# Joins of the weights' conversion moved behind masking and low parts in a linear-attention and two-MoE kernel

## The chip, the cores and the metric

The kernel runs on one core of a Trainium2 chip. The metric is the time in microseconds that the device takes for one execution; the median of three runs is compared. Names of engines in the rows: PE is TensorE's matmul and PEld its weight load, DVE is VectorE, ACT is ScalarE, POOL is GpSimd, SP is SyncE, which issues most of the transfers.

## What is computed

Three stages follow each other. A linear attention with decay (2 batches, 8 heads, 768 steps, head dimension 48) gives 1536 rows of 384. A feed-forward layer with a leaky activation (384 to 2048 to 384) follows, and then a routed layer with 8 experts (384 to 1024 to 384), each token going to its best expert. Only the first two stages are touched by the change:

```python
for t in range(S):
    kt, vt, rt = (k[:, :, t], v[:, :, t], r[:, :, t])
    cur = np.einsum('bhd,bhe->bhde', u[None] * kt, vt)
    y[:, :, t] = np.einsum('bhd,bhde->bhe', rt, state + cur)
    state = w[None, :, :, None] * state + np.einsum('bhd,bhe->bhde', kt, vt)
...
h = x @ w_in
g = np.maximum(h, 0.0) + alpha * np.minimum(h, 0.0)
return (g @ w_out).astype(np.float32)
```

## The kernel before

The 1536 tokens are cut into 12 tiles of 128 and three blocks of four tiles. Attention of the first four tiles runs ahead; then the feed-forward layer goes over block 0, 1 and 2, each in 16 slices of 128 hidden units (so 48 slices), and the attention of the next block's tiles is threaded into the slices of the block before it. In each slice `moe1_slice` has TensorE make nine products into a PSUM bank h (three passes over high and low parts, L608), ScalarE scales and clips them into ng (L624), VectorE multiplies and adds (L627), ScalarE casts the high part gh (L628), VectorE subtracts to get the low part gl (L631). The slice then runs the second product (L593, twelve matmuls) of the slice two before. There are two banks h, so the first products of slice g wait for gl of slice g - 2.

Every product takes float32 numbers as a high and a low part. For the weights these parts are made on the chip, once, by `convert_moe1`: 256 hidden units make one q (0 to 7), part 0 is the first layer's weight, part 1 the second layer's. A conversion has six steps:

- step 0 (L359): ScalarE scales the high words into the scratch tile rowss
- step 1: nothing
- step 2 (L362): VectorE shifts and masks in rowss
- step 3 (L365), the first join: VectorE brings in bits of the low words, still in rowss
- step 4 (L368), the second join: VectorE puts the number together in the raw weight tile rm
- step 5: ScalarE casts the high part into wm (L371) and GpSimd subtracts to get the low part there (L372)

From q = 4 on all conversions use the same half of rowss, so step 0 of one waits for step 4 of the one before.

The order in each queue is that in which the code is written out; nothing reorders it. A slice has five places for other work: its start, behind ng, behind gh, behind gl, and behind the second product. The table CONVERT gives, for the conversion whose base slice is `at` (2q for part 1, 2q - 3 for part 0), six numbers, one for each step: number p means slice at + p // 5, and p % 5 is the place in the order just named. A conversion without an entry takes OTHERS. At one place the conversion's steps come first and the attention's behind them. The attention of a tile has phases in fixed slices: the score is made and masked (L213 and L216, `score0`, behind gh) in slices 2, 5, 8 and 11; the finished tile is transposed (px, L265, end of slices 5, 8, 13 and 14) and put into xh and xl (L273, L274, start of the next). The score's two banks, px, pr (L186), pk (L198), py (L222, L229) and pg (L240) share two banks of PSUM in turn.

Of the kernel before, what the change touches and what calls it, by code (L numbers as in the profile page):

```python
# [23 lines left out]
def kernel(  # L24
# [918 lines left out]
    with tc.manual_schedule():  # L943
# [137 lines left out]
        c1[5]()  # L1081


        CONVERT = {0: (0, 0, 0, 0, 2, 3), 1: (-5, 1, 1, 1, 5, 9), 2: (-4, -2, -1, 2, 3, 7), 4: (-1, 0, 2, 5, 6, 7), 5: (-4, -1, 0, 1, 4, 6), 3: (-4, 0, 2, 5, 5, 7), 6: (-3, -1, 2, 4, 5, 7), 7: (-6, -6, -4, -2, 2, 4)}
        OTHERS = (-1, -1, 0, 0, 0, 5)
        work = [([], [], [], [], [], []) for _ in range(NBLK * NFT)]
        for q in range(NW):
            for x in range(2):
# [5 lines left out]
                def step(n, c=c, q=q, x=x):  # L1094
                    if n == 0:
                        c.extend(convert_moe1(q, x, nc.gpsimd))
                    c[n]()
                for n, p in enumerate(CONVERT.get(at, OTHERS)):
                    g = at + p // 5
# [144 lines left out]
```

## Time and profile before

| what | us |
|---|---|
| median of three runs | 464.07 |
| lowest and highest run | 461.83, 465.22 |
| the profiled execution | 462.03 |
| its span on the core | 459.9 |
| TensorE busy in the span | 424.0 (92%) |
| VectorE busy in the span | 267.9 (58%) |
| ScalarE busy in the span | 201.7 (44%) |
| GpSimd busy in the span | 160.0 (35%) |

Durations in the profile come from the one profiled execution, whose time stands beside its span; the 2.1 us between them lie around the span. The shares are means over stages with different limits, so a stage is read from windows of its own.

### The profile page before, as it was taken

The page shows a single profiled execution, that of the slowest core. Times are in us where ns is not written, and L with a number is a line of the kernel's source. Part 1 is how long each engine was busy: PE and PEld are TensorE (multiplying, and loading weights), DVE is VectorE, ACT ScalarE, POOL GpSimd, SP SyncE. Part 2 cuts the span into 40 slices and gives each one's busy share as a digit, 9 for nine tenths or more (in the row PEclk, how much of TensorE's full clock was granted, in tenths as well). Part 3 has the DMA queues.
Part 4 walks back from the last instruction along what each step waited for, and adds up shares of the span by engine and source line. Part 5 has one row for each costly group of instructions (what it writes and reads, how often), then busy time and mean ns, then how long its engine had stood idle before and what let it go on. Part 6 is the DMA issues. An engine that isn't in the chain of part 4 may idle for free. (4 is left out here: it accounts for less than half of the span.)

```text
span 459.9 us, 7878 instructions
## 1 busy us (share of the span) xinstructions
PE 424.0 (92%) x3012; PEld 363.5 (79%) x3012; DVE 267.9 (58%) x475; ACT 201.7 (44%) x335; POOL 160.0 (35%) x141
## 2 busy tenths in 40 slices
PE   8877989699899999999999999999998887899985
PEld 7765778488788988988898889987966465798774
DVE  6888998999753444345433575354535355443651
ACT  1236545354444333323254444334636366543861
POOL 7845467454440231100300040031407145521660
PEclk9998999989999999999999999999999899899999
DMA  7989950649610105200900020016748728901900
GB/s 130 231 250 280 337 149 3 169 145 358 205 36 17 38 16 201 92 0 6 340 1 1 0 75 12 1 45 192 285 148 281 261 62 298 323 34 41 323 16 19
DMA packets 70513, 62.36 MB, mean 136 GB/s; under 512 B 41837, under 2 KB 58131, under 8 KB 70464
## 3 DMA queue, kind: packets, MB, share of 16 engines
q1 hardware_dynamic: 68832, 57.29, 40.4%
q0 software_dynamic: 1632, 4.40, 2.5%
q8 instruction: 32, 0.52, 0.5%
q14 instruction: 17, 0.14, 0.1%
HBM read 49.99 MB, written 12.18 MB: 135 GB/s over the span
## 5 line engine op out<-in xcount | busy, mean ns | idle before, releaser
L593 PE MATMUL acc<-wm,gh 128*128 128x384 f32 x384 | 100.8, 343 | 0.5 <-POOL wm L372 0.5
L608 PE MATMUL h<-xh,wm 128*128 128x512 f32 (+1 forms) x294 | 87.4, 407 | 3.6 <-DVE gl L631 3.6
L627 DVE SCALAR_TENSOR_TENSOR h<-ng,sign,h 128x512 f32<-128x512 f32 x48 | 36.1, 752 | 67.9 <-ACT ng L624 67.9
L593 PEld LDWEIGHTS acc<-wm,gh 128*128 128x128 f32 x384 | 68.8, 188 | 4.9 <-POOL wm L372 1.1
L593 PE MATMUL acc<-wm,gl 128*128 128x384 f32 x192 | 64.8, 338 | 0.0
L608 PEld LDWEIGHTS h<-xh,wm 128*128 128x128 f32 x294 | 53.2, 192 | 13.3 <-issue 2.9
L788 PE MATMUL eh<-we,d 128*128 128x512 f32 x198 | 54.5, 420 | 5.4 <-ACT we L687 3.1
L690 POOL TENSOR_TENSOR we<-re,we 128x768 fp32r<-128x768 f32 x21 | 41.7, 1984 | 50.8 <-ACT we L687 36.0
L624 ACT ACTIVATE ng<-h,slope 128x512 f32<-128x512 f32 x48 | 33.1, 690 | 57.3 <-PE h L608 57.3
L628 ACT CAST gh<-h 128x512 fp32r<-128x512 f32 x48 | 28.1, 586 | 63.3 <-DVE h L627 63.3
L687 ACT CAST we<-re 128x768 fp32r<-128x768 f32 x64 | 50.6, 839 | 1.8 <-ACTq L934 1.4
L690 DVE TENSOR_TENSOR we<-re,we 128x768 fp32r<-128x768 f32 x43 | 40.7, 973 | 17.8 <-ACT we L687 16.8
L788 PEld LDWEIGHTS eh<-we,d 128*128 128x128 f32 x198 | 37.2, 197 | 17.3 <-issue 9.9
L372 POOL TENSOR_TENSOR wm<-rm,wm 128x768 fp32r<-128x768 f32 x16 | 32.2, 2012 | 46.8 <-ACT wm L371 42.9
L526 POOL DMA_INDIRECT disp<-rows,sl x12 | 12.6, 1048 | 100.0 <-DVE run L552 64.4
L608 PE MATMUL h<-xl,wm 128*128 128x512 f32 (+1 forms) x147 | 42.9, 401 | 0.0
L631 DVE TENSOR_TENSOR gl<-h,gh 128x512 fp32r<-128x512 f32 x48 | 33.0, 687 | 15.6 <-ACT gh L628 15.0
L805 DVE TENSOR_TENSOR gl<-pht,gh 128x512 fp32r<-128x512 f32 x22 | 15.2, 692 | 44.1 <-ACT gh L804 42.4
L813 PE MATMUL ey<-we,gh 128*128 128x384 f32 x176 | 37.7, 346 | 0.0
L593 PEld LDWEIGHTS acc<-wm,gl 128*128 128x128 f32 x192 | 36.1, 188 | 0.0
L608 PEld LDWEIGHTS h<-xl,wm 128*128 128x128 f32 x147 | 28.2, 194 | 6.9 <-DVE xl L274 0.2
L813 PEld LDWEIGHTS ey<-we,gh 128*128 128x128 f32 x176 | 29.7, 189 | 0.4 <-ACT gh L804 0.4
(200 smaller groups left out, 612.8 us busy)
## 6 DMA issues: line engine op xcount, KB each, us to landing
re<-in_moe_w_dram SPq DMA_DIRECT2D x32, 768.0 KB, 6.6
rm<-in_moe_w_in_dram SPq DMA_DIRECT2D x8, 768.0 KB, 5.9
rm<-in_moe_w_out_dram SPq DMA_DIRECT2D x8, 768.0 KB, 6.7
disp<-rowss SPq DMA_DIRECT2D x1, 4825.0 KB
drow<-disp SPq DMA_DIRECT2D x7, 579.0 KB, 8.2
out_dram<-rowss SPq DMA_DIRECT2D x1, 2304.0 KB, 22.7
kn<-in_k_dram SPq DMA_DIRECT2D x10, 192.0 KB, 7.6
rn<-in_r_dram SPq DMA_DIRECT2D x10, 192.0 KB, 3.6
```

What stands on the lines that cost most here:

```text
L372: eng.tensor_tensor(lo, low.bitcast(F32), hi.bitcast(F32), ALU.subtract)
L593: nc.tensor.matmul(accs[(blk, s)], gs[g][a][:, s * P:(s + 1) * P], wout[b][:, ft % 2, :], start=(ft == 0 and n == 0), stop=(ft == NFT - 1 ...
L608: nc.tensor.matmul(phs[g][:, cols[0]:cols[1]], win[a][:, c, o:o + P], xs[b][:, c, cols[0]:cols[1]], start=(n == 0), stop=(n == 3 * DC - 1))
L624: nc.scalar.activation(ng, ph, AF.Relu, scale=slope[:, ft:ft + 1])
L627: nc.vector.scalar_tensor_tensor(ph, ng, sign[:, ft:ft + 1], ph, op0=ALU.mult, op1=ALU.add)
L628: nc.scalar.copy(gh, ph)
L631: nc.vector.tensor_tensor(gl, ph, gh.bitcast(F32), ALU.subtract)
L687: nc.scalar.copy(t[:, sl], src[:, sl])
L690: le.tensor_tensor(t[:, sl2], src[:, sl], t[:, sl].bitcast(F32), ALU.subtract)
L788: nc.tensor.matmul(ph[q], d[x][:, c, :], ww[y][:, c, :], start=(n == 0), stop=(n == 3 * DC - 1))
L805: nc.vector.tensor_tensor(hl, pt, hh.bitcast(F32), ALU.subtract)
L813: nc.tensor.matmul(py, hT[q][x][:, c * P:(c + 1) * P], ww[y][:, c, :], start=(q == 0 and not low and c == 0 and y == 0), stop=(q == 1 and ...
```

## The change

Five entries of the table are changed or new. Entry 0 (second layer's weight of q 0) puts its two joins behind gl of slice 0 and at the end of that slice, and step 5 behind ng of slice 1. Entry 1 (q 2, part 0) puts its first join behind gl of slice 1. Entry 4 (q 2, part 1) puts its first join at the end of slice 4 and its second at the start of slice 5. Entry 5 (q 4, part 0) puts its first join behind gl of slice 5, and so behind the masking. Entries 8 and 11 (q 4 part 1, q 7 part 0) had taken OTHERS, with both joins at the start of slice 8 or 11 and step 5 at the start of the next; now the first join stands behind gl, the second behind the first or at the slice's end, and step 5 behind the next slice's ng.

```diff
-        CONVERT = {0: (0, 0, 0, 0, 2, 3), 1: (-5, 1, 1, 1, 5, 9), 2: (-4, -2, -1, 2, 3, 7), 4: (-1, 0, 2, 5, 6, 7), 5: (-4, -1, 0, 1, 4, 6), 3: (-4, 0, 2, 5, 5, 7), 6: (-3, -1, 2, 4, 5, 7), 7: (-6, -6, -4, -2, 2, 4)}
+        CONVERT = {0: (0, 0, 0, 3, 4, 6), 1: (-5, 1, 1, 3, 5, 9), 2: (-4, -2, -1, 2, 3, 7), 4: (-1, 0, 2, 4, 5, 7), 5: (-4, -1, 0, 3, 4, 6), 3: (-4, 0, 2, 5, 5, 7), 6: (-3, -1, 2, 4, 5, 7), 7: (-6, -6, -4, -2, 2, 4),
+                   8: (-1, -1, 0, 3, 4, 6), 11: (-1, -1, 0, 3, 3, 6)}
```

VectorE in slice 0, before (rm_164 is the raw tile of q 0, h_0 and gl_0 are slice 0's):

```order
L362 TENSOR_SCALAR rowss<-rowss 128x768
L365 SCALAR_TENSOR_TENSOR rowss<-rm_164,rowss 128x768
L627 SCALAR_TENSOR_TENSOR h_0_524<-ng_0_564,sign,h_0_524 128x512
L368 SCALAR_TENSOR_TENSOR rm_164<-rm_164,rowss 128x768
L631 TENSOR_TENSOR gl_0_566<-h_0_524,gh_0_565 128x512
L251 TENSOR_TENSOR Sc<-pg_534,Sc 128x192
L252 TENSOR_TENSOR Sc<-Sc,w_100 128x192
L192 TENSOR_TENSOR rT_588<-pr_578,tabE 128x512
```

The same place now:

```order
L362 TENSOR_SCALAR rowss<-rowss 128x768
L627 SCALAR_TENSOR_TENSOR h_0_524<-ng_0_563,sign,h_0_524 128x512
L631 TENSOR_TENSOR gl_0_565<-h_0_524,gh_0_564 128x512
L365 SCALAR_TENSOR_TENSOR rowss<-rm_164,rowss 128x768
L368 SCALAR_TENSOR_TENSOR rm_164<-rm_164,rowss 128x768
L251 TENSOR_TENSOR Sc<-pg_534,Sc 128x192
L252 TENSOR_TENSOR Sc<-Sc,w_100 128x192
L192 TENSOR_TENSOR rT_586<-pr_576,tabE 128x512
```

The two joins of rm_164 stand behind gl, no longer around the multiplication L627.

ScalarE in slices 0 and 1, before (wm_288 is the converted tile of q 0, kT and S belong to the attention of tile 4):

```order
L624 ACTIVATE ng_0_564<-h_0_524,slope 128x512
L628 CAST gh_0_565<-h_0_524 128x512
L371 CAST wm_288<-rm_164 128x768
L254 COPY S_118<-Sc 64x4x48 x2
L206 COPY kT_590<-pk_583 128x512
L624 ACTIVATE ng_1_605<-h_1_595,slope 128x512
L359 ACTIVATE rowss<-rm_172 128x768
```

The same place now:

```order
L624 ACTIVATE ng_0_563<-h_0_524,slope 128x512
L628 CAST gh_0_564<-h_0_524 128x512
L254 COPY S_118<-Sc 64x4x48 x2
L206 COPY kT_588<-pk_581 128x512
L624 ACTIVATE ng_1_603<-h_1_593,slope 128x512
L371 CAST wm_288<-rm_164 128x768
L359 ACTIVATE rowss<-rm_172 128x768
```

The cast L371, from which GpSimd's subtraction follows, has moved behind S, kT and ng of slice 1.

VectorE in slices 8 and 9, before (rm_551 is the raw tile of q 4, rm_745 that of q 6):

```order
L362 TENSOR_SCALAR rowss<-rowss 128x768
L365 SCALAR_TENSOR_TENSOR rowss<-rm_551,rowss 128x768
L368 SCALAR_TENSOR_TENSOR rm_551<-rm_551,rowss 128x768
L627 SCALAR_TENSOR_TENSOR h_8_988<-ng_8_998,sign,h_8_988 128x512
L216 TENSOR_TENSOR A_1004<-pa_0_1005,upper 128x512
L216 TENSOR_TENSOR A_1004<-pa_1_1006,upper 128x512
L631 TENSOR_TENSOR gl_8_1000<-h_8_988,gh_8_999 128x512
L274 TENSOR_TENSOR xl_863<-px_1037,xh_862 128x3x128
L362 TENSOR_SCALAR rowss<-rowss 128x768
L365 SCALAR_TENSOR_TENSOR rowss<-rm_745,rowss 128x768
L368 SCALAR_TENSOR_TENSOR rm_745<-rm_745,rowss 128x768
L627 SCALAR_TENSOR_TENSOR h_9_1048<-ng_9_1058,sign,h_9_1048 128x512
```

The same place now:

```order
L362 TENSOR_SCALAR rowss<-rowss 128x768
L627 SCALAR_TENSOR_TENSOR h_8_986<-ng_8_996,sign,h_8_986 128x512
L216 TENSOR_TENSOR A_1002<-pa_0_1003,upper 128x512
L216 TENSOR_TENSOR A_1002<-pa_1_1004,upper 128x512
L631 TENSOR_TENSOR gl_8_998<-h_8_986,gh_8_997 128x512
L365 SCALAR_TENSOR_TENSOR rowss<-rm_550,rowss 128x768
L368 SCALAR_TENSOR_TENSOR rm_550<-rm_550,rowss 128x768
L274 TENSOR_TENSOR xl_863<-px_1037,xh_862 128x3x128
L362 TENSOR_SCALAR rowss<-rowss 128x768
L365 SCALAR_TENSOR_TENSOR rowss<-rm_745,rowss 128x768
L368 SCALAR_TENSOR_TENSOR rm_745<-rm_745,rowss 128x768
L627 SCALAR_TENSOR_TENSOR h_9_1046<-ng_9_1056,sign,h_9_1046 128x512
```

The multiplication, the two masks and gl of slice 8 stand ahead of both joins of q 4, and these directly ahead of xl and q 6's steps.

## Rows read from the trace of the kernel before

**Rows 1.** Windows of the span: per engine busy us (instructions); then clock, DMA share, GB/s.

```profile
40.00:48.00 8.00, 6.48 (x34) 5.16 (x35) 7.28 (x10) 5.38 (x9) 5.87 (x4) 0.79 0.99 279
...
88.00:96.00 8.00, 4.48 (x17) 3.23 (x15) 7.89 (x9) 2.60 (x4) 3.81 (x2) 0.81 0.55 195
...
136.00:144.00 8.00, 8.00 (x44) 7.00 (x43) 3.26 (x5) 3.98 (x8) 0.00 (x0) 1.00 0.13 25
```

**Rows 2.** Waits over the whole span: total us, times, longest us.

```profile
ACT rowss L359 <- DVE rm L368: 5.9, 3, 2.4
...
PE px L265 <- DVE A L216: 5.1, 2, 3.5
```

**Rows 3.** Groups by line: busy us, mean ns, then idle before and releasers.

```profile
L627 DVE SCALAR_TENSOR_TENSOR h<-ng,sign,h 128x512 f32<-128x512 f32 x48 | 36.1, 752 | 67.9 <-ACT ng L624 67.9
...
L628 ACT CAST gh<-h 128x512 fp32r<-128x512 f32 x48 | 28.1, 586 | 63.3 <-DVE h L627 63.3
...
L372 POOL TENSOR_TENSOR wm<-rm,wm 128x768 fp32r<-128x768 f32 x16 | 32.2, 2012 | 46.8 <-ACT wm L371 42.9 <-DVE rowss L362 3.8
...
L368 DVE SCALAR_TENSOR_TENSOR rm<-rm,rowss 128x768 int32<-128x768 int32 x16 | 25.3, 1584 | 0.3
...
L365 DVE SCALAR_TENSOR_TENSOR rowss<-rm,rowss 128x768 int32<-128x768 int32 x16 | 21.5, 1350 | 0.3
...
L362 DVE TENSOR_SCALAR rowss<-rowss 128x768 int32<-128x768 int32 x16 | 14.0, 872 | 3.8 <-ACT rowss L359 3.7
```

**Rows 4.** Timeline, slices 0 to 3: start us, length us, engine, [idle <-releaser].

```profile
36.74 1.52 DVE L362 TENSOR_SCALAR rowss<-rowss 128x768 int32<-128x768 int32 x1 [1.32 <-ACT rowss L359]
...
38.29 0.96 DVE L365 SCALAR_TENSOR_TENSOR rowss<-rm,rowss 128x768 int32<-128x768 int32 x1
...
40.69 0.68 DVE L631 TENSOR_TENSOR gl<-h,gh 128x512 fp32r<-128x512 f32 x1
...
41.52 1.43 PE L608 MATMUL h<-xh,wm 128*128 128x512 f32 x3 [2.45 <-DVE gl L631]
...
41.77 1.98 POOL L372 TENSOR_TENSOR wm<-rm,wm 128x768 fp32r<-128x768 f32 x1 [3.94 <-ACT wm L371]
...
45.33 1.16 PE L213 MATMUL pa<-rT,kT 64*128 64x128 f32 x16
...
46.43 0.62 PE L593 MATMUL acc<-wm,gh 128*128 128x384 f32 x2
...
48.65 0.86 PE L608 MATMUL h<-xh,wm 128*128 128x512 f32 x3
```

**Rows 5.** Timeline, slices 5 to 7.

```profile
69.02 0.55 PE L265 MATMUL px<-ident,cv 128*128 128x128 f32 x3 [1.56 <-DVE A L216]
...
70.54 2.04 DVE L368 SCALAR_TENSOR_TENSOR rm<-rm,rowss 128x768 int32<-128x768 int32 x1
...
73.91 0.56 DVE L274 TENSOR_TENSOR xl<-px,xh 128x384 fp32r<-128x384 f32 x1 [1.33 <-ACT xh L273]
...
75.00 0.95 PE L608 MATMUL h<-xh,wm 128*128 128x512 f32 x3
```

**Rows 6.** Timeline, slices 8 to 10.

```profile
87.56 2.56 POOL L372 TENSOR_TENSOR wm<-rm,wm 128x768 fp32r<-128x768 f32 x1
...
88.45 2.49 DVE L368 SCALAR_TENSOR_TENSOR rm<-rm,rowss 128x768 int32<-128x768 int32 x1
...
92.25 0.55 PE L265 MATMUL px<-ident,cv 128*128 128x128 f32 x3 [3.52 <-DVE A L216]
...
96.34 1.14 PE L229 MATMUL py<-v,A 128*64 128x48 f32 x32
...
97.01 1.66 DVE L368 SCALAR_TENSOR_TENSOR rm<-rm,rowss 128x768 int32<-128x768 int32 x1
...
100.06 0.60 PE L186 MATMUL pr<-ident,rn 128*128 128x128 f32 x4
```

**Rows 7.** Timeline, slices 12 to 14.

```profile
116.08 2.52 DVE L368 SCALAR_TENSOR_TENSOR rm<-rm,rowss 128x768 int32<-128x768 int32 x1
...
120.66 0.73 PE L608 MATMUL h<-xh,wm 128*128 128x512 f32 x2 [1.17 <-DVE gl L631]
```

## The prediction, made before the changed kernel ran

> **What bounds the kernel now.** The table of windows comes first, because shares over the whole span mix stages [rows 1]. From 136 us on TensorE is busy in all of 8.00 us: there, time lost earlier stays lost and nothing is won back. Before that it isn't TensorE: between 88 and 96 us VectorE is busy for 7.89 of 8 us and TensorE for 4.48, at a mean granted clock of 0.81 (1 is 2.4 GHz; a product then runs in part at the half level, 1.2). So while the weights are converted (slices 0 to 14 of block 0, about 33 to 128 us) VectorE's queue sets the pace, and TensorE's waits are its symptom. The view of waits says where they show: TensorE waits 5.1 us in two places for the masking, at the transposes px, which take over the score's bank, and ScalarE waits 5.9 us in three places at the conversion's first step (L359) for its last step on VectorE (L368) [rows 2]: both use the one scratch tile rowss. The groups by line give VectorE's load [rows 3]. The three steps take 0.87, 1.35 and 1.58 us on average. A step L365 that meets nobody takes 0.96 [rows 4], and L362 and L368 are about 0.55 and 0.95 alone (worked out from the held pairs below). 16 conversions thus hold some 60.8 - 16 x 2.46 = 21 us of waiting inside instructions. What holds them is GpSimd's subtraction: the L368 at 88.45 meets an L372 that ends at 87.56 + 2.56 = 90.12 and ends itself at 90.94, 0.82 later [rows 6]. The L362 at 36.74 is held likewise [rows 4].
>
> The Trainium skill (SBUF — State Buffer, Who interferes with whom) says that a VectorE instruction with two SBUF inputs and a GpSimd instruction that reads SBUF shut each other out for the whole instruction. L365 and L368 have two such inputs, and the pair at 88.45 agrees, with 0.82 us left to do once the other ends. By that rule alone it matters whom a moved join meets, not how far it moves; that is the rival named "the lock" below.
>
> **How the cost is worked out.** I walk the five queues forward in their new order from 36 us, each instruction with its length alone (rows), L362, L365 and L368 ending 0.4, 0.8 and 0.8 us after a subtraction of GpSimd that they meet, GpSimd starting when such a step is through, and nine products in 2.1 us at full clock. Walked so, the old order brings slice 14's products at 120.5, where the trace has 120.66 [rows 7]; so a difference between two walks of under half a microsecond says nothing. No transfer is moved: the step that issues loads (the first of a conversion) stays, and SP's queue is unchanged; the load in slice 8 that waits for a subtraction of GpSimd comes some 2 us later, two slices before it is used.
>
> **Slice 0 (entry 0).** L365 leaves the head of slice 0. The multiplication L627 then follows L362, which ends at 38.26, instead of L365 [rows 4]: it starts at 38.2 and takes 0.75, the cast L628 0.59 [rows 3], so gl starts at 39.6 in place of 40.69, and slice 2's products at 40.4 in place of 41.5: 1.1 us won. TensorE then idles 1.4 us and not 2.45, less than the 1.56 us at 69.02 [rows 5] after which the granted clock stayed at 1.00. So the half clock that follows in the trace (window 40 to 48 at 0.79, that is 0.21 x 8 = 1.7 us) should go as well: 2.8 us by the end of these products. But then something else is late. VectorE now idles while gl waits for its cast, so the two joins and the state come later: rT 0.8 us later, and the scores start at 44.1 (45.3 before). And the entry's last step moves from slice 0 to slice 1: ScalarE's L371 for wm now stands behind kT and slice 1's ng, it ends at 45.4, and GpSimd's L372 runs from 45.5 to 47.3 instead of from 41.77 [rows 4]. The second product of slice 0 reads that low part; it could start at 45.5 (46.43 before) but its third matmul waits for GpSimd until 47.4. Slice 3 starts at 49.3 in place of 48.65: 0.7 us later, with everything won in slice 0 gone.
>
> **Slices 1 to 7 (entries 1, 4 and 5).** In slice 1 L365 goes behind gl, where a kd of GpSimd holds it (ends at 49.1), and the next L368 ends 0.4 us later than before. In slice 5, L365 of entry 5 goes behind the masking, which thereby gains 0.95 us on the rest: px, waiting until 69.02 in the trace [rows 5], comes at 69.7, late by 0.6 and no longer by 1.4. But that L365 now stands between gl and L368. L365 meets wm's subtraction and L368 meets the next GpSimd operation: L368 ends at 74.6 in place of 72.58. ScalarE's next L359 waits for it (scratch tile), xh stands behind L359, so xl comes at 76.0 and not at 73.91, and pk, whose bank xl frees, waits. Slice 7 starts at 77.1 in place of 75.00: 2.1 us late.
>
> **Slices 8 to 10 (entry 8).** Here the change does most. The trace has L365 and L368 ahead of the masking, the second held until 90.94; TensorE waits 3.52 us and then runs at half clock (window at 0.81, 1.5 us) [rows 1, 6]. Now L627 and the masks come straight after L362: px at 90.6 in place of 92.25, in spite of a start 2.1 us late, and the nine products at full clock, so that py could start at 93.0 in place of 96.34: 3.3 us ahead. It is given back in three steps. L368 now ends at 93.3, so that L359, xh and xl follow it (xl from 94.7) and TensorE waits 1.4 us for the bank. Entry 8's last step moved behind slice 9's ng, so wm's subtraction runs from 96.1 to 98.4 and meets the next L368, which ends at 99.2 in place of 98.67. Behind that stand slice 9's L627 and the sum cv, which frees pr's bank: pr at 100.5, in place of 100.06. TensorE idles 2.4 us there. Net: 0.4 us late.
>
> **Slices 11 to 14 (entry 11).** L365 and L368 go behind the masking and gl; they meet nobody, where L368 had been held, and 1.5 us of holding go. But L359 of the next conversion waits for that L368 until 114.6, so L362 starts at 115.6, and VectorE idles 1 us ahead of it. Slice 12's ng, behind L359 on ScalarE, comes at 115.5, L371 for wm behind that, GpSimd's subtraction runs from 117.1 to 118.9, and the L368 which in the trace ends at 116.08 + 2.52 = 118.60 [rows 7] ends at 119.7. Slice 12's L627 and gl follow, and slice 14's products start at 121.9 in place of 120.66. From there on all is TensorE's, and the 1.2 us stay.
>
> **The sum.** VectorE runs the same instructions up to that gl in either order. Held time inside them falls in the walk from 19.6 to 15.6 us, VectorE's idle time grows from 5.5 to 10.7: -4.0 + 5.2 = +1.2 us; against the old order's own walk the whole is +1.4. I take +1.3 us. On the profiled execution, 462.03 us, that is 463.3. That execution lies 2.0 us under the median of 464.07, inside the runs' own spread (461.83 to 465.22); the change on the median gives 465.4. Varying every length by 1.5% and the handovers by 0.03 us moves the sum between +1.0 and +1.8.
>
> **Rivals.** *The lock*: only the meetings with GpSimd count, the idle time doesn't grow, since ScalarE's first steps are ready when VectorE comes. Then the 4.0 us of held time are won: 460.1. For it speaks that VectorE's idle time is small now; against it, that ScalarE already waits 5.9 us for L368 [rows 2] and the change puts L368 later at every place. *Everything seen is won*: the waits and half clocks in slices 2, 6 and 9 go for good, 2.45 + 1.7 + 1.56 + 3.52 + 1.5 = 10.7 us, 453.3. Against it: VectorE would have to do its load in less than it has. *The clock*, which ends slower: the wait ahead of slice 14 grows from 1.17 us [rows 7] to 2.4. In the trace 2.45 us was followed by half clock and 1.56 wasn't [rows 4, 5]; if 2.4 is enough, 1.2 to 1.7 us are lost where TensorE is the bound: 466.8. The same wait at slice 10 costs little, since VectorE sets the pace there. The Trainium skill (TensorE: Matmul & The Clock Gate, What's actually happening) says that the clock follows how busy the engine has lately been, and that the moment of change differs from run to run; no run here shows the second, and it would make this rival a matter of the run. *Nothing moves*: the queue of VectorE is full either way and gains and losses cancel, 464.1.
>
> **How the numbers follow.** One per cent is 4.6 us, about what a measurement of this kernel can tell from no change. Chances: forecast 0.47, clock 0.24, nothing 0.17, lock 0.08, everything won 0.04. The first four lie within one per cent of 464.07; the runs' spread of 1.7 us to a side and a walk that misses one meeting with GpSimd (2.0 us [rows 3]) can carry the clock's case over it, 0.06, and the lock's under it, 0.02. So faster 0.06, same 0.88, slower 0.06. The range takes in forecast, clock and nothing with that spread: 461.8 to 468.6, leaving out the lock and everything won.
>
> **What would show it.** Right: gl of slice 0 near 39.6 and TensorE's next products at full clock; a new wait of TensorE for L372 of about 1.7 us in slice 2; the longest wait for the masking gone, from 3.5 us to under 1.5; ScalarE's wait at L359 for L368 well over 5.9 us; slice 14's products near 122; held time of L368 down and VectorE's idle time up between 33 and 122. Wrong: slice 14's products before 119, which would mean that ScalarE is ready for VectorE after all, or after 124, which would mean a meeting with GpSimd that the walk doesn't see.

## The result, and the profile after

| what | before | changed |
|---|---|---|
| median, us | 464.07 (20 runs, 460.60 to 465.22) | 466.25 (20 runs, 463.52 to 469.26) |
| ratio, 95% interval | 1 | 1.0059 (1.0040 to 1.0077) |
| a second job: median, us | 463.10 (29 runs) | 464.18 (12 runs, 461.45 to 467.04) |
| its ratio, 95% interval | 1 | 1.0021 (0.9989 to 1.0053) |
| profiled executions, us | 462.03 | 463.88, and 464.54 in the second job |
| slice 14's first products start at, us | 120.66 | 122.17, and 121.79 in the second job |

By the two jobs the changed kernel is slower by 0.2 to 0.6%, inside the 1% that was called no change; the first interval leaves out a ratio of 1, the second doesn't. From slice 14 on, both traces of it run parallel to the one of before, late by 1.51 and 1.13 us. Slice 1's products, which start ahead of everything that the change moves, already lie at +0.19 and -0.19 us, so between slices 1 and 14 both traces lose 1.32 us.

Windows of the changed kernel, in the columns of [rows 1]:

```profile
40.00:48.00 8.00, 4.18 (x27) 2.91 (x27) 5.53 (x10) 4.62 (x8) 2.42 (x3) 0.88 0.96 271
48.00:56.00 8.00, 8.00 (x30) 7.44 (x31) 8.00 (x10) 2.90 (x4) 2.65 (x2) 0.69 1.06 363
88.00:96.00 8.00, 6.50 (x66) 5.27 (x67) 6.61 (x10) 4.04 (x7) 3.97 (x3) 1.00 0.58 199
96.00:104.00 8.00, 5.82 (x40) 5.16 (x36) 7.49 (x10) 3.82 (x7) 6.45 (x6) 0.80 0.37 114
...
36.90:122.10 85.20, 74.30 (x505) 63.56 (x503) 75.77 (x91) 41.12 (x65) 43.89 (x30) 0.94 0.67 209
```

The dip of 88 to 96 us in [rows 1] is gone (TensorE busy 6.50 us in place of 4.48, clock 1.00), and a smaller one stands 8 us later (5.82, clock 0.80). In 48 to 56 us TensorE is busy throughout, at 0.69. The last row reaches from VectorE's first L362 to slice 14's products.

Waits over the whole span, as in [rows 2], and groups, as in [rows 3]:

```profile
ACT rowss L359 <- DVE rm L368: 14.9, 5, 3.5
```

```profile
PE pr L186 <- DVE cv L232: 2.2, 1, 2.2
PE acc L593 <- POOL wm L372: 1.9, 2, 1.4
...
PE px L265 <- DVE A L216: 0.3, 1, 0.3
```

```profile
L372 POOL TENSOR_TENSOR wm<-rm,wm 128x768 fp32r<-128x768 f32 x16 | 30.4, 1901 | 50.0 <-ACT wm L371 49.9
...
L368 DVE SCALAR_TENSOR_TENSOR rm<-rm,rowss 128x768 int32<-128x768 int32 x16 | 22.6, 1412 | 0.4
L365 DVE SCALAR_TENSOR_TENSOR rowss<-rm,rowss 128x768 int32<-128x768 int32 x16 | 20.4, 1280 | 0.1
...
L362 DVE TENSOR_SCALAR rowss<-rowss 128x768 int32<-128x768 int32 x16 | 12.7, 791 | 3.9 <-ACT rowss L359 3.7
```

TensorE's waits for the masking fell from 5.1 to 0.3 us and VectorE's three steps from 60.8 to 55.7 us; ScalarE's waits for L368 rose from 5.9 to 14.9 us.

Timeline of the changed kernel, slices 0 to 3:

```profile
38.36 0.74 DVE L627 SCALAR_TENSOR_TENSOR h<-ng,sign,h 128x512 f32<-128x512 f32 x1
...
39.75 0.69 DVE L631 TENSOR_TENSOR gl<-h,gh 128x512 fp32r<-128x512 f32 x1 [0.65 <-ACT gh L628]
...
40.59 0.94 PE L608 MATMUL h<-xh,wm 128*128 128x512 f32 x3 [1.33 <-DVE gl L631]
...
44.44 1.16 PE L213 MATMUL pa<-rT,kT 64*128 64x128 f32 x16 [1.52 <-ACT kT L206]
...
45.96 1.85 POOL L372 TENSOR_TENSOR wm<-rm,wm 128x768 fp32r<-128x768 f32 x1 [5.58 <-ACT wm L371]
...
47.86 0.69 PE L593 MATMUL acc<-wm,gh 128*128 128x384 f32 x1 [1.38 <-POOL wm L372]
...
51.55 1.05 PE L608 MATMUL h<-xh,wm 128*128 128x512 f32 x2
```

Slice 2's products come 0.93 us before [rows 4] and at full clock (0.94 us for three, in place of 1.43). Two waits of 1.5 and 1.4 us that were not there follow, and then half clock: the products at 47.86 take twice their time, and slice 3 comes at 51.55 in place of 48.65.

Slices 5 to 7:

```profile
70.05 0.55 PE L265 MATMUL px<-ident,cv 128*128 128x128 f32 x3 [0.35 <-DVE A L216]
...
71.56 2.04 DVE L365 SCALAR_TENSOR_TENSOR rowss<-rm,rowss 128x768 int32<-128x768 int32 x1
...
73.64 1.47 DVE L368 SCALAR_TENSOR_TENSOR rm<-rm,rowss 128x768 int32<-128x768 int32 x1
...
75.15 0.89 ACT L359 ACTIVATE rowss<-rm 128x768 f32<-128x768 f32 x1 [3.50 <-DVE rm L368]
...
76.44 0.56 DVE L274 TENSOR_TENSOR xl<-px,xh 128x384 fp32r<-128x384 f32 x1 [1.33 <-ACT xh L273]
...
77.53 0.95 PE L608 MATMUL h<-xh,wm 128*128 128x512 f32 x3
```

The wait for the masking is 0.35 us ([rows 5]: 1.56). But both joins are held by GpSimd, ScalarE waits 3.50 us for the second, and xl and slice 7 are 2.5 us late.

Slices 8 to 10:

```profile
91.08 0.49 PE L265 MATMUL px<-ident,cv 128*128 128x128 f32 x3
...
92.82 0.96 DVE L368 SCALAR_TENSOR_TENSOR rm<-rm,rowss 128x768 int32<-128x768 int32 x1
...
93.60 1.14 PE L229 MATMUL py<-v,A 128*64 128x48 f32 x32
93.81 0.92 ACT L359 ACTIVATE rowss<-rm 128x768 f32<-128x768 f32 x1 [3.10 <-DVE rm L368]
...
95.14 0.56 DVE L274 TENSOR_TENSOR xl<-px,xh 128x384 fp32r<-128x384 f32 x1 [1.36 <-ACT xh L273]
...
96.58 2.31 POOL L372 TENSOR_TENSOR wm<-rm,wm 128x768 fp32r<-128x768 f32 x1 [4.61 <-ACT wm L371]
...
97.19 2.51 DVE L368 SCALAR_TENSOR_TENSOR rm<-rm,rowss 128x768 int32<-128x768 int32 x1
...
100.88 1.11 PE L186 MATMUL pr<-ident,rn 128*128 128x128 f32 x4 [2.18 <-DVE cv L232]
```

py comes 2.7 us before its place in [rows 6]; pr, which follows pg and the second product, 0.8 us behind its own.

Slices 12 to 14:

```profile
115.06 0.90 ACT L359 ACTIVATE rowss<-rm 128x768 f32<-128x768 f32 x1 [3.06 <-DVE rm L368]
...
116.00 0.56 DVE L362 TENSOR_SCALAR rowss<-rowss 128x768 int32<-128x768 int32 x1 [0.97 <-ACT rowss L359]
...
117.42 1.87 POOL L372 TENSOR_TENSOR wm<-rm,wm 128x768 fp32r<-128x768 f32 x1 [5.46 <-ACT wm L371]
...
117.59 2.52 DVE L368 SCALAR_TENSOR_TENSOR rm<-rm,rowss 128x768 int32<-128x768 int32 x1
...
122.17 0.96 PE L608 MATMUL h<-xh,wm 128*128 128x512 f32 x3 [0.29 <-DVE gl L631]
```

L368 ends at 120.11 ([rows 7]: 118.60), since L359 waited 3.06 us for the L368 before it. And TensorE itself is late here: it waits only 0.29 us for gl ([rows 7]: 1.17), because it has worked without a pause since pr at 100.88, the first 3.4 us at half clock.

### The profile page after: what moved, and what is told of

The parts are those of the page before. It is cut to its first block, busy times and chain, and to the rows that moved or that the text cites. A ratio compares the mean times of both kernels' runs of the same rounds, so it can differ in the third digit from the quotient of the medians.

```text
span 461.8 us, 7880 instructions
## 1 busy us (share of the span) xinstructions
PE 423.6 (92%) x3012; PEld 364.0 (79%) x3012; DVE 263.6 (57%) x475; ACT 202.1 (44%) x335; POOL 158.0 (34%) x141
## 5 line engine op out<-in xcount | busy, mean ns | idle before, releaser
L593 PE MATMUL acc<-wm,gh 128*128 128x384 f32 x384 | 102.4, 347 | 2.2 <-POOL wm L372 1.9
L627 DVE SCALAR_TENSOR_TENSOR h<-ng,sign,h 128x512 f32<-128x512 f32 x48 | 36.1, 753 | 70.1 <-ACT ng L624 70.1
L593 PEld LDWEIGHTS acc<-wm,gh 128*128 128x128 f32 x384 | 69.9, 190 | 7.1 <-POOL wm L372 2.8
L788 PE MATMUL eh<-we,d 128*128 128x512 f32 x198 | 52.9, 410 | 4.6 <-ACT we L687 2.4
L788 PEld LDWEIGHTS eh<-we,d 128*128 128x128 f32 x198 | 36.1, 191 | 15.7 <-issue 8.8
L372 POOL TENSOR_TENSOR wm<-rm,wm 128x768 fp32r<-128x768 f32 x16 | 30.4, 1901 | 50.0 <-ACT wm L371 49.9
L526 POOL DMA_INDIRECT disp<-rows,sl x12 | 12.6, 1049 | 101.5 <-DVE run L552 64.4
L608 PE MATMUL h<-xl,wm 128*128 128x512 f32 (+1 forms) x147 | 41.8, 392 | 0.5 <-DVE xl L274 0.5
```

The costliest lines, as they stand in the source:

```text
L372: eng.tensor_tensor(lo, low.bitcast(F32), hi.bitcast(F32), ALU.subtract)
L593: nc.tensor.matmul(accs[(blk, s)], gs[g][a][:, s * P:(s + 1) * P], wout[b][:, ft % 2, :], start=(ft == 0 and n == 0), stop=(ft == NFT - 1 ...
L608: nc.tensor.matmul(phs[g][:, cols[0]:cols[1]], win[a][:, c, o:o + P], xs[b][:, c, cols[0]:cols[1]], start=(n == 0), stop=(n == 3 * DC - 1))
L627: nc.vector.scalar_tensor_tensor(ph, ng, sign[:, ft:ft + 1], ph, op0=ALU.mult, op1=ALU.add)
L788: nc.tensor.matmul(ph[q], d[x][:, c, :], ww[y][:, c, :], start=(n == 0), stop=(n == 3 * DC - 1))
```

## The experiments

All ratios are to the kernel before, on the same chip in the same job, with 95% intervals; d1, d3, d9, d10 and d14 are how much later than in the trace of before the first products of slices 1, 3, 9, 10 and 14 start, in us. Each is read from one profiled execution. The first instruction that any of these kernels moves or adds starts later than slice 1's products (36.73 us in the trace of before; L365, the first to move, is at 38.29 [rows 4]), so d1 is only a difference between executions, and the last column takes it off. The change has six changed or new entries (0, 1, 4, 5, 8 and 11), not five; 1, 4, 5 and 11 were not run by themselves.

| run | ratio | d1 | d3 | d9 | d10 | d14 | d14 less d1 |
|---|---|---|---|---|---|---|---|
| the change | 1.0059 (1.0040 to 1.0077) | +0.19 | +2.90 | -1.22 | +1.65 | +1.51 | +1.32 |
| the change again | 1.0021 (0.9989 to 1.0053) | -0.19 | +2.52 | -1.57 | +0.60 | +1.13 | +1.32 |
| entry 8 alone | 0.9970 (0.9940 to 0.9999) | -0.13 | -0.17 | -3.91 | -1.81 | -1.46 | -1.33 |
| entry 0 alone | 0.9996 (0.9974 to 1.0018) | -0.10 | +2.63 | +1.39 | +1.39 | +1.39 | +1.49 |
| change, two scratch halves | 1.0002 (0.9979 to 1.0025) | -0.05 | +2.66 | -1.42 | -0.81 | -0.08 | -0.03 |
| entry 8, two scratch halves | 0.9941 (0.9908 to 0.9974) | -0.08 | -0.12 | -3.89 | -3.25 | -2.68 | -2.60 |
| change, kept busy | 0.9992 (0.9972 to 1.0012) | -0.15 | +0.94 | -1.58 | +0.53 | +1.15 | +1.30 |
| change, kept busy, again | 0.9964 (0.9932 to 0.9995) | -0.45 | +0.63 | -1.95 | +0.14 | +0.85 | +1.30 |
| change, cast in slice 0 | 1.0046 (1.0017 to 1.0075) | -0.16 | -1.21 | -1.98 | +0.13 | +0.87 | +1.03 |
| before, kept busy | 0.9979 (0.9953 to 1.0006) | -0.17 | -0.89 | -0.23 | -0.23 | -0.25 | -0.08 |
| 14 entries, two scratch halves | 0.9841 (0.9812 to 0.9869) | -0.67 | -0.75 | -8.41 | -8.68 | -10.06 | -9.39 |
| 14 entries, one scratch half | 0.9841 (0.9814 to 0.9868) | +0.56 | -1.00 | -6.78 | -7.23 | -8.66 | -9.22 |
| best table | 0.9738 (0.9704 to 0.9773) | +0.30 | +0.26 | -7.74 | -8.63 | -10.01 | -10.31 |

**Entry 8 alone.** All other entries as before.

```diff
+ 8: (-1, -1, 0, 3, 4, 6)
```

> Entry 8 of the change alone (both joins behind the masking of slice 8, last step behind the next slice's ng); the other four entries as before. Theory 'queue' (VectorE's queue sets the pace until slice 14, and a moved join is worth what it wins at the masking minus what the steps behind it lose): slice 9's first products about 4.0 us earlier than before, slice 10's only 1.8 us earlier, because the scratch tile keeps ScalarE's L359 behind the moved L368 and the later subtraction of GpSimd holds the next L368; slice 14's products and the end 1.1 us earlier, ratio 0.9975. Rival 'clock' (the changed kernel loses by TensorE's half clock alone, 10.2 us of it up to slice 11 against 6.8 us before): here slice 2's half clock stays as before and slice 9's goes, so 1.7 us are won and kept at slice 10, 0.996, without any give-back between slices 9 and 10.

Slices 9, 10 and 14 came at -3.91, -1.81 and -1.46 us. So the part of the change that attacks the longest wait of [rows 2] gains, and gives more than half of it back within one slice, as the walk had it.

**Entry 0 alone.**

```diff
- 0: (0, 0, 0, 0, 2, 3)
+ 0: (0, 0, 0, 3, 4, 6)
```

> Entry 0 of the change alone (joins of the first weight behind gl of slice 0, last step behind ng of slice 1). 'Queue': slice 2's products about 1 us earlier, slice 3's at least 0.7 us later through the wait for GpSimd's subtraction, and 0.5 us of that left at slice 14: ratio 1.001. 'Clock': the half clock of 6.8 us that the changed kernel shows from slice 2 on is there with entry 0 alone, 3.4 us more than before, and costs 1.7 us or more up to slice 14: ratio 1.004.

Slice 3 is 2.63 us late in the trace, and half clock lasts 6.8 us there as in the change; at slice 14 +1.39 us are left, where the theory of the queues had 0.5. Over the runs no loss shows, within 0.2%; the trace is of the slowest of the 12 runs (465.31 us). The half clock in slices 2 and 3 is thus entry 0's, but a loss by it isn't shown.

**The change with q 4's second part in the other half of the scratch tile.** It takes away what L359 waits for in slice 9.

```diff
-        at = part * n if 2 * q < 8 else 0
+        at = part * n if 2 * q < 9 else 0
```

> The change, with one more edit: the conversion of q 4, part 1 uses the other half of the scratch tile, so ScalarE's L359 of q 6 no longer waits for the moved L368 in slice 8. 'Queue': everything up to slice 9 as in the changed kernel, then slice 10's products 1.5 us earlier than there, slice 14's as before the change: ratio 1.000 to the kernel before, against 1.006 of the change. 'Clock' and the theory that the scratch tile is no part of it: no difference from the changed kernel.

Slice 10 comes 2.46 us before that of the changed kernel (-0.81 against +1.65), slice 14 1.59. Of the 2.46 us, 0.24 are there at slice 1, and a part is half clock, which the changed kernel's trace has from 100.7 us on. What the wait costs is read ahead of that, from VectorE's sum cv in slice 9, here and in the changed kernel:

```profile
98.60 0.54 DVE L232 TENSOR_TENSOR cv<-py,cv 128x384 f32<-128x384 f32 x1
```

```profile
100.28 0.55 DVE L232 TENSOR_TENSOR cv<-py,cv 128x384 f32<-128x384 f32 x1
```

That is 1.68 us, or 1.44 without the difference at slice 1. At slice 14 the loss is gone in the trace, from one wait removed, and the ratio is 1.0002. This run also prices the rival called the clock: here TensorE waits 1.85 us for gl ahead of slice 14, half clock follows at 121 us, and slice 15 is at +0.88: 0.96 us lost.

**Entry 8 alone with the same edit of the scratch.**

> Entry 8 alone, and the conversion of q 4, part 1 in the other half of the scratch tile. 'Queue': slice 9's products 4.0 us earlier than before, of which 3.3 stay at slice 10 and 2.6 at slice 14: ratio 0.994, faster than both kernels. If the scratch tile is no part of it: as entry 8 alone, 0.9975.

Waits of this kernel, and of entry 8 alone behind it:

```profile
ACT rowss L359 <- DVE rm L368: 5.9, 3, 2.4
```

```profile
ACT rowss L359 <- DVE rm L368: 9.0, 4, 3.1
```

The wait that entry 8 adds (9.0 against the 5.9 of before) is the one in slice 9, 3.1 us long, and the second half of the scratch takes it away. Slice 10 comes at -3.25 in place of -1.81 us, 1.44 us earlier again, and cv (97.60 us with entry 8 alone) at 96.16. The ratio is 0.9941: faster than the kernel before and the changed one.

**The change with TensorE kept busy in slice 2.** 17 products are added in two places of slice 2, 8 behind gh and 9 behind gl, and overwritten later.

```diff
+    def busy(n):
+        win = moe1_w(0)[0]
...
+        for _ in range(n):
+            nc.tensor.matmul(accs[(0, 0)], win[0][:, 0, 0:P], xT[0][0][:, 0, 0:DM], start=True, stop=True)
```

> The changed kernel with 17 products added in slice 2 (128x384, into a bank of the accumulator that is written afresh later, 8 ahead of the score and 9 ahead of the second product), so that TensorE is busy in the two waits after which its clock fell to half for 6.8 us (46.2 to 53.0 us of the changed kernel). Theory, VectorE's queue sets slice 14: the half clock in slices 2 and 3 is gone or shorter, slice 3 comes some 2 us earlier than in the changed kernel, and slice 14's products stay at +1.5 us to the kernel before, the ratio to it at 1.002 to 1.007. Rival, the clock: the changed kernel loses through the half clock, 1.7 us or more are won at slice 14 too (about -0.2 us to the kernel before) and the ratio falls to 0.999 or lower.

The half clock is gone there and slice 3 comes at +0.94, 2.0 us before the changed kernel's. Slice 14 moved by 0.36 us only, as the theory of the queues has it, and 0.34 of these are there at slice 1 already; but the ratio fell to 0.9992, as the rival has it. Both kernels were run again, on one chip:

> The changed kernel itself, on the same chip as the next two, for a second trace of it and a comparison with the kernel that keeps TensorE busy in slice 2. Theory, the queues alone (walk +1.4 us at slice 14): ratio 1.001 to 1.005, the first result of 1.0059 partly chance, and the kept-busy kernel would come to the same if run beside it. Rival, queues and clock: 1.004 to 1.008, with more half clock in the mean of the runs (mean granted clock 0.979 to 0.980 against 0.982 of the kernel before).

> The changed kernel with the 17 added products in slice 2 once more, beside the changed kernel on one chip. Theory, the queues alone: within 0.002 of the changed kernel. Rival, the clock has a part: 0.004 to 0.009 below the changed kernel, a mean granted clock over the runs of 0.985 to 0.987, and slice 14's products earlier than in the changed kernel's trace by more than the 0.36 us seen so far.

The medians were 464.18 and 462.24 us, ratios 1.0021 and 0.9964, mean granted clocks over the runs 0.982 and 0.987. The gap of 0.0057 between the ratios (2.6 us) is in line with the first, 0.0067 (3.1 us), though each ratio of the second job is known to 0.003 only: the kept-busy kernel really is faster, by some 2 to 3 us. Yet the second pair of traces shows 0.28 us of that at slice 14, and 0.26 of these at slice 1. Counted from slice 1, all four traces of the changed and the kept-busy kernel, with half clock in slices 2 and 3 or without, come to slice 14 at +1.30 to +1.32 us. Windows of the kept-busy kernel, second trace, and its slice 14:

```profile
40.00:48.00 8.00, 7.57 (x47) 6.40 (x48) 5.52 (x9) 4.63 (x8) 2.69 (x2) 1.00 1.00 292
48.00:56.00 8.00, 8.00 (x45) 7.24 (x44) 8.00 (x11) 2.77 (x5) 2.03 (x2) 1.00 1.03 345
...
96.00:104.00 8.00, 5.84 (x34) 5.11 (x33) 7.40 (x10) 4.10 (x7) 6.94 (x7) 1.00 0.46 148
```

```profile
121.51 0.97 PE L615 MATMUL h<-xh,wm 128*128 128x512 f32 x3 [1.86 <-DVE gl L640]
```

This trace has no half clock at all between 32 and 136 us, TensorE waits 1.86 us for VectorE's gl ahead of slice 14 (its line is L640 in this kernel), and slice 14 still comes at +0.85, which is +1.30 counted from slice 1. That is the part of VectorE's queue alone, and it is the whole loss of the changed kernel's traces up to there.

**The change with the cast back in slice 0.** Entry 0's step 5 stands right behind its second join.

```diff
- 0: (0, 0, 0, 3, 4, 6)
+ 0: (0, 0, 0, 3, 4, 4)
```

> The changed kernel with one number of entry 0 changed back in sense: its step 5 (the cast L371 and GpSimd's L372) at the end of slice 0, right behind the second join, no longer behind ng of slice 1. Theory, the queues: the second product in slice 2 no longer waits for L372 (1.7 us in the changed kernel), slice 3 comes before its place in the kernel before (-1.0 us, +0.8 with half clock), but slice 14's products are late as in the changed kernel (+1.4 us), since the two later places where VectorE idles for L359 are unchanged: ratio 1.002 to 1.006. Rival: the wait for L372 in slice 2 is what costs; then slice 14 comes at +0.0 to +0.3 us and the ratio is 1.000.

Slice 3 comes 1.21 us before that of before, 4.1 us before the changed kernel's, and slice 14 at +0.87 (+1.03 counted from slice 1, against +1.32), with a ratio as in the change. The new wait for L372 in slice 2 isn't what costs the change its time, but for 0.3 us by these traces.

**The kernel before with TensorE kept busy** in its wait of 2.45 us ahead of slice 2's products [rows 4].

```diff
+        if g == 2:
+            busy(12)
         ph = moe1_first(g, (2 * P, N) if g == 0 else (0, N))
```

> The kernel before with 12 products added ahead of slice 2's products (128x384, into a bank of the accumulator that is written afresh later), in its wait of 2.45 us for gl of slice 0, so that the 3.4 us at half clock behind it should go. Theory, the queues: VectorE sets the pace up to slice 14, the 1.7 us are won in slice 2 and gone at slice 14 (under 0.4 us there), ratio 0.999 to 1.001. Rival, the clock has a part here too: 1.0 to 1.7 us at slice 14, ratio 0.996 to 0.998.

```profile
40.00:48.00 8.00, 6.99 (x44) 5.57 (x43) 7.28 (x10) 5.22 (x9) 5.84 (x4) 1.00 1.00 283
```

```profile
120.41 0.97 PE L615 MATMUL h<-xh,wm 128*128 128x512 f32 x3 [1.15 <-DVE gl L640]
```

The window has its full clock ([rows 1]: 0.79). Slice 3 comes 0.89 us earlier and slice 14, at 120.41, 0.25 us, of which 0.17 are there at slice 1: what was won in slice 2 is gone again by slice 14. The ratio, 0.9979 (0.9953 to 1.0006), reaches to both theories.

**Tables written with the walk.** Two of 14 entries came first:

> A table of conversions written with the walk of the queues (14 entries; entry 0 as before, entry 8 as changed, entries 1 to 7 and 11 new, first joins of 9, 10 and 12 earlier) and q 4's part 1 in the other half of the scratch tile. Theory, the queues of VectorE, ScalarE and GpSimd set the pace up to slice 14, and where VectorE neither idles nor is held there is time to win: slice 9's products at -8.7 us, slice 14's at -11 us, the ratio 0.975 to 0.98. Rival, the bound is TensorE itself by then (half clock after its waits, or its own load): no more than the 3.5 us of entry 8 with two scratch halves is won, ratio 0.992 to 0.995.

> The same 14 entries with the scratch tile as it is in both kernels. Theory, the queues: slice 9's products at -8.7 us, slice 10's at -8.6, slice 14's at -10 us, ratio 0.977 to 0.982, 1.1 us behind the kernel with the second half of scratch. Rival, the scratch tile is what limits any such table: under 6 us at slice 14, ratio 0.987 or higher.

In both, q 4's first-layer weights are other numbers, since its second join reads scratch that q 5 has already written; the tokens are then routed otherwise (216 products L788 of the routed layer in the trace, 198 before), and of the 10.7 and 9.3 us that they are ahead at the end of block 2 their spans keep 5.6 and 5.4. They show the order's speed up to slice 14 (walk -11 and -10, trace -10.06 and -8.66, or -9.39 and -9.22 counted from slice 1: the second half of the scratch is worth 0.2 us here and not the 1.1 that were expected), and nothing of the end. The table that keeps each half of the scratch in order:

```diff
+ CONVERT = {0: (0, 0, 0, 0, 2, 3), 1: (-5, 1, 1, 2, 3, 9), 2: (-4, -2, 2, 2, 3, 8),
+   3: (-4, 0, 2, 3, 5, 7), 4: (-1, 0, 2, 5, 6, 6), 5: (-4, -1, 0, 1, 4, 6),
+   6: (-3, -1, 1, 5, 7, 7), 7: (-6, -6, -4, -2, 2, 4), 8: (-1, -1, 0, 3, 4, 5),
+   9: (-1, -1, -1, 0, 3, 6), 10: (-1, -1, 0, 0, 0, 5), 11: (-1, -1, 0, 2, 2, 9),
+   12: (-1, -1, 0, 2, 2, 6), 14: (-1, -1, 0, 0, 0, 5)}
+ at = part * n if 2 * q < 9 else 0
```

> A table like the one of the two kernels with 14 entries and q 4's part 1 in the other half of the scratch tile, in which no conversion begins in a half of the scratch before the one ahead of it has left that half (the two tables of 14 entries tried before broke this at q 4's part 0: its second join came behind the first step of q 5's part 0). Theory, the queues: slice 9's products at -8.4 us, slice 14's at -10.6 us, and the ratio as for those two, 0.98 to 0.985. Rival, what those two won came from the broken order: no more than the 3.7 us of entry 8 with two scratch halves, ratio 0.991 to 0.995.

```profile
64.00:72.00 8.00, 7.47 (x46) 6.58 (x43) 6.66 (x11) 4.44 (x8) 4.40 (x3) 1.00 0.25 49
...
88.00:96.00 8.00, 7.79 (x63) 6.93 (x59) 7.58 (x10) 4.80 (x9) 6.15 (x6) 1.00 0.55 181
```

```profile
L368 DVE SCALAR_TENSOR_TENSOR rm<-rm,rowss 128x768 int32<-128x768 int32 x16 | 18.9, 1186 | 0.2
```

It takes 450.40 us, 0.9738 of before: slice 14 comes at -10.01 us (walk -10.6). The ratio is lower than the 0.98 to 0.985 expected; in the trace a further 2.1 us are won behind block 2, which the walk doesn't reach. TensorE is busy for 7.79 us between 88 and 96, some eight to nine us further on in the work ([rows 1]: 4.48), and the L368 are held 0.4 us less each ([rows 3]: 1584 ns), with ScalarE's wait for them at 8.3 us in five places, the longest 2.0.

## Why the prediction was right, and where it was not

**The mechanism and the sum.** VectorE's 91 instructions from the first L362 to slice 14 hold it 75.77 us of 85.20. The like window in the trace of before:

```profile
36.70:120.60 83.90, 73.09 (x505) 61.80 (x503) 79.92 (x91) 40.96 (x65) 45.79 (x30) 0.96 0.69 213
```

So busy time, the held time with it, fell by 4.15 us and idle time rose by 5.45, +1.30; predicted were -4.0 and +5.2. The time rose by 2.2 us in the medians of the first job and 1.1 in the second, around the forecast of 1.3; behind block 2 the changed kernel's two traces lose another 0.3 and 1.3 us, which no term of the sum has. *Everything seen is won* and *nothing moves* are refuted by the traces, and *the lock*, by which idle time doesn't grow, by entry 8 alone: of the 3.91 us that it won at slice 9 it kept 1.81 at slice 10, and ScalarE's wait of 3.1 us for L368 is new there. That this wait takes back the gain is shown by taking it away: 1.44 us come back, with entry 8 alone (-1.81 became -3.25) and, at cv, in the change. The lock itself is real: the L368 at 97.19 ends 0.81 us after the L372 at 96.58 does. The Trainium skill (SBUF — State Buffer, Who interferes with whom) says that a VectorE instruction with two SBUF inputs and a GpSimd instruction that reads SBUF contend, and the trace agrees.

**Slice 0.** L627, gl and slice 2's products came within 0.2 us of the walk, at full clock. The step that failed is "So the half clock that follows in the trace [...] should go as well": it moved 4 us on and became twice as long, 46.1 to 52.9 us. Of the waits of the new order that the prediction itself lists (1.4 us, one for the scores, one for L372) only the first was compared with the wait of 1.56 us that had no half clock behind it. With TensorE kept busy, slice 3 comes at 49.58 and 49.27, where the prediction had 49.3, so the rest of that paragraph held. The miss didn't reach the sum: slice 14 comes 1.30 us late without that half clock and 1.32 with it, counted from slice 1.

**Slices 1 to 7.** px, L368's end, xl and slice 7 were forecast at 69.7, 74.6, 76.0 and 77.1, and came at 70.05, 75.11, 76.44 and 77.53: all 0.35 to 0.5 us late by about one amount. About 0.2 us of that is this execution's start (L362 at 36.95 in place of 36.74), and the rest is within the half microsecond that the walk claims. The half clock in slices 2 and 3 isn't it: counted from slice 1, slice 7 is 2.34 us late in both traces with it, and 2.32 and 2.25 in the two without.

**Slices 8 to 10.** px 90.6 (91.08), py 93.0 (93.60), xl from 94.7 (95.14), L372 from 96.1 (96.58), next L368's end 99.2 (99.70), pr 100.5 (100.88): the three steps of giving back, in their order and sizes. Slice 10's products are 1.65 us late, 0.8 of it because pr and pk behind it run at half clock from 100.7 us on. That costs little at slice 14, as the prediction said: the kept-busy kernel has 3.4 us of half clock there in one trace and none in the other, and slice 14 is at +1.30 in both, counted from slice 1.

**Slices 11 to 14.** L359 waits until 115.06 (114.6), VectorE idles 0.97 us (1), L372 starts at 117.42 (117.1), L368 ends at 120.11 (119.7), slice 14 at 122.17 (121.9).

**The clock as a rival** was put at the wrong place. The wait ahead of slice 14 was 0.29 us and not 2.4, since TensorE was late itself; no half clock followed there. Where such a wait did occur (1.85 us, the change with two scratch halves), it cost 0.96 us, under the 1.2 to 1.7 that were forecast; a wait of 1.86 us at the same place, in the second kept-busy trace, had no half clock behind it.

What the runs leave open is the 2 to 3 us that the kept-busy kernel wins over the changed one. By the runs the added products win them, but the traces show none of it up to slice 14. Entry 0 alone has the same half clock in its trace and, over the runs, a like mean granted clock (0.980, as in the first job of the change), and it loses nothing there. Over the 232 runs for which a clock was kept, counted within each kernel, an execution is 0.23 us shorter for each 0.001 more of mean granted clock; the 0.005 between the two kernels would by that be worth 1.2 us, an estimate from runs that weren't made to differ. In the changed kernel's trace TensorE and VectorE arrive at slice 14 within 0.29 us of each other, so a further stretch at half clock between 100 and 122 us would cost there in full; that some executions have one is argued, not shown. The routed stage can hold a part: from the end of block 2 to the end of the run the changed kernel lost 0.3 us to before in one trace and 1.3 in the other, the kept-busy kernel lost 0.1 and won 0.2. The Trainium skill (TensorE: Matmul & The Clock Gate, What's actually happening) says that the moment of a change of clock differs from run to run; the two traces of the kept-busy kernel agree: 3.4 us at half clock from 101.5 us on in the first, none there in the second.

## What to carry to other kernels

Before a step is moved behind other work, list who waits for its last write, through shared scratch as well, and what stands behind that waiter in its queue: here a gain of 3.9 us at TensorE shrank to 1.8 within a slice, and a second half of scratch gave 1.4 of it back. When one engine's queue sets the pace, write out all queues with measured durations and choose the whole table with that; moving single steps away from the longest visible wait gave between +0.6% and -0.3%, a table chosen as a whole, with the second half of scratch for one conversion, -2.6%. Compare the traces at the last place where the change can act, since the executions' ends differ by more than the change does, and count from the last place where it can't yet: here that made 1.51, 1.13, 1.15 and 0.85 us one number, 1.3.

## What was not expected of the hardware

Three waits of TensorE of 1.33, 1.52 and 1.38 us within 8 us (ends at 40.59, 44.44 and 47.86) went with 6.8 us at the lower level of the clock, while the single one of 1.56 us [rows 5] had none behind it; the other three traces with entry 0's late cast and nothing put into the waits show the same, and filling the last two waits with products removed it. From the end of block 2 on, which no table here touches, the kernels that route alike took from 2.1 us less (the best table) to 2.4 us more (entry 8 alone) than the trace of before, both with two stretches of 3.4 us at half clock there and the last 1.5 and 3.1 us, like before with 1.7.
